# Three attention chunks in step, reordered loads, masks ahead of low parts, late conversions behind a fixed unit

## The chip, the cores and the metric

The kernel runs on one core of a Trainium2 chip. A core has five engines that run their own instruction streams and wait for each other by semaphores: TensorE (PE, matrix multiplications into accumulation banks), VectorE (DVE), ScalarE (ACT), GpSimd (POOL) and SyncE (SP, which here issues the transfers). The metric is device time in microseconds (us) of one launch; the kernel before takes 869.1 us, the median of three runs (868.42 to 871.12).

## The reference

Three stages follow one another, all in f32:

```python
f = 1 / (1 + exp(-f_logit))                     # 4 x 8 heads, 768 steps, 48 dims
for t in range(S):
    state = f[:, :, t, :, None] * state + einsum('bhd,bhe->bhde', k_t, v_t)
    y[:, :, t] = einsum('bhd,bhde->bhe', q_t, state)
x = y as 3072 tokens x 384
h = x @ w_in                                    # 384 -> 2048
x = where(h > 0, h, exp(min(h, 0)) - 1) @ w_out # 2048 -> 384
out = ((x @ w1) * (x @ w2) @ w3) @ w_out2       # 384 -> 1024 -> 1024 -> 384
```

Weights and inputs reach the kernel as 64-bit floats, in pairs of 32-bit words, and are converted on the chip.

## The kernel before

**Tiles.** The gated linear attention is cut into 24 chunks of 128 tokens (6 a batch), the first MLP into 8 tiles of 384 tokens, three chunks a tile. A tile has 16 *units* m, one for each 128 of the 2048 hidden columns; unit U = 16 j + m. In the order of the program, unit U holds `p1_split` of the unit before (the high part gh on ScalarE, L658, and the low part gl on VectorE, L659), the in-matmuls `p1_in` (9 in tiles 1 to 7, L640), the ELU (ScalarE L643 and L644, VectorE L646 into g) and the out-matmuls `p1_out` of unit U - 2 (9 or more, L672; after unit 15 the results leave by L681). Tile 0 runs in plain f32, the others as products of high and low parts.

**Attention.** Attention of tile j + 1 runs inside tile j. A chunk passes through the steps a_clamp, b0 to b5 and a4: clamp (L332), log of the gate (L351, L352), scan (L357), exponentials (L364, L365), scaling of key and query (L373, L374, on GpSimd for chunks 1 and 2) and a copy of the decay (L375), scores (L383) and transposes of the key (L389) on TensorE, masks on VectorE (L397, twice a chunk) and the copy of the transposed key on ScalarE (L399), then the output (L444), its high and low part (L453, L455) and the state (L408, L422 to L428). `ATT_AT` and `ATT_OFF` say at which units of the tile the three chunks' steps stand: masks in units 6, 10 and 14, the output right behind the in-matmuls of the same unit. For tile 0 `ATT_AT0` and `ATT_OFF0` do the same. The chunks of tile 0 itself are done in the prologue, in the order of `PRO_ORDER`: a code is the chunk and its step (k the last one), w a number of warm-up multiplications of zeros, j a conversion step. `PRO_LOADS` gives the order of the loads there on SP (l weights, d query and key, v values).

**Conversions.** A weight piece is loaded into a staging tile (wst, four buffers, L492), its magnitude is summed on ScalarE (L226, `cv_abs`), VectorE rebuilds the word (L230, L231, L236), and high and low part are split off. Conversions of w3 and w_out2 for the second MLP are spread over units 32 to 104 and go out to memory (L554, L560, L562). Those of w1 and w2 are the late jobs, `job_12`, in tile 7, and reuse the tile wa7 of the spilled ones.

**What sets the order.** The prologue and the units from `MAN` = 17 to `MAN_B` = 110 are in the order in which the code is written; everywhere else a scheduler places each instruction when the tiles that it needs are ready by its own estimate, so that it may put a job's first instruction ahead of units that come before it in the code. Every engine runs its stream in order. The w_out product (`w_rows`, L725) follows from unit 117 on, its operands o2 and w3 loaded by SP (L703, L713) behind the late jobs' loads.

Of the kernel before, what the change touches and what calls it, by code (L numbers as in the profile page):

```python
# [9 lines left out]
F32 = mybir.dt.float32  # L10
F32R = mybir.dt.float32r
U32 = mybir.dt.uint32
# [28 lines left out]
CPT = TN // CH  # L41
NTILE = NT // TN
# [7 lines left out]
Y_ROUNDS = ((0, 0, ((0, 0),)), (1, 64, ((80, 1),)), (2, 32, ((32, 0), (48, 1))))  # L50
ATT_AT = (0, 4, 8)
ATT_OFF = (0, 1, 2, 3, 4, 5, 6, 6)
ATT_AT0 = (0, 5, 9)
ATT_OFF0 = (0, 0, 1, 2, 3, 3, 4, 5)
ST_BUFS = 4
EARLY = (0, 1, 2, 3, 4, 6)
P2_Q = 1
SPILL_AT = 2 * MF
PRO_LOADS = "l d0 d1 l v0 v1 d2 l l v2 l l l"
PRO_ORDER = "w19 00 10 01 02 11 12 03 13 04 20 14 21 05 22 15 23 0k 1k j 06 j 16 24 25 2k 26"  # L60
BANKS = ("aaaaa", "hh0aa", "12aaa")
MAN = 17
Q_POOL = (1, 2)
# [184 lines left out]
def main_path(ctx, tc, flag, qkf, vin, w_in, w_out, w1, w2, w3T, w_out2, ident_d, tri_d, x2_scr, o2_scr, w3_scr, out):  # L248
    nc = tc.nc
# [3 lines left out]
    wp = ctx.enter_context(tc.tile_pool(name="wp", bufs=1))  # L253
# [13 lines left out]
    keep = tri_f.bitcast(U32).unsqueeze(1).to_broadcast([128, NP, CH])  # L267
# [21 lines left out]
    def carve(name, dt, *cols):  # L289
        t = wp.tile([128, KD * 512], dt, name=name)  # L290
        o = np.cumsum((0,) + cols)
        return [t[:, int(a):int(b)] for a, b in zip(o, o[1:])]

    def by_pair(t):
        return t.rearrange("r (p t) -> r p t", p=NP)
# [4 lines left out]
    for c, (x, y) in enumerate((("wb4", "wb5"), ("wb6", "wb7")), 1):  # L300
        e, k = carve(x, F32, 512, 512)
# [4 lines left out]
    def buf(c, nm, make):  # L306
        return own[c][nm] if c < CPT and nm in own[c] else make()
# [35 lines left out]
    def khc(c):  # L343
        return buf(c, "kh", lambda: kh)

    def amats(c):
        return buf(c, "amat", lambda: amat)
# [43 lines left out]

    c_ps = {}

    def b5(c):
        ps = c_ps.pop(c)
        for e in range(2):
            nc.vector.copy_predicated(out=amats(c)[e], mask=keep, data=by_pair(ps[e]))  # L397
        if len(ps) > 2:
            nc.scalar.activation(out=khc(c).rearrange("t p r -> t (p r)"), in_=ps[2][:, 0:NP * PR], func=AF.Copy)  # L399

    def a4k(c):
        if c % CPB == CPB - 1:
            return
        v = cx[c]["v"]
        kp = bank(c, 4)
        for i in range(NP):
            for e, (r, cc) in enumerate(blocks):
                nc.tensor.matmul(kp[r, 2 * D * i:2 * D * (i + 1)][:, cc], lhsT=khc(c)[:, i, r],  # L408
                                 rhs=v[:, i, V_AT[e]:V_AT[e] + D], start=True, stop=True)
        c_kp[c] = kp  # L410
# [65 lines left out]
    late = {}  # L476
# [18 lines left out]
    def cv_abs():  # L495
        i = cv["abs"]
        if i < cv["load"]:
            cv["abs"] += 1
            n, _, dst, place = jobs[i]
            src = cvt[i][0][:, 0:n, :]  # L500
            if place is None:
                if "wt" not in late:
                    late["wt"] = wp.tile([128, 3 * 512], U32, name="wa7")
                x = i % 4
                t = late["wt"][:, 512 * x:512 * x + n] if x < 3 else cv_p.tile([128, 512], U32, name="wt")[:, 0:n]
            else:
                t, groups = place()
                src = src.rearrange("p (a n) two -> p a n two", a=groups)
            cvt[i] = (src, t)
            rebias(nc, src, t, total[:, i:i + 1])  # L510
# [8 lines left out]
    def cv_step(k=1):  # L519

        while cv["split"] < cv["main"]:
            cv_split()
        i = cv["main"]
        k = min(k, len(jobs) - i)
        while cv["load"] < i + k:
            cv_load()
        while cv["abs"] < i + k:
            cv_abs()
        cv["main"] += k
        rebiased_to_f32(nc, [cvt[x] for x in range(i, i + k)])  # L530
        while cv["load"] < min(i + k + ST_BUFS - 2 + (3 if i < 2 * MF - 8 else 0), len(jobs)):
            cv_load()
        while cv["abs"] < min(cv["load"], i + k + (2 if i < 2 * MF else 1)):
            cv_abs()
# [226 lines left out]
    for m in range(MF + LAG):  # L761
        if m < MF:
            job_1(m, 0)
        if m >= LAG:
            job_1(m - LAG, 1)
    for code in PRO_LOADS.split():
        if code == "l":
# [12 lines left out]
    def fill():  # L780
# [4 lines left out]
        quota[0] = 0  # L785

    steps = (a_clamp, b0, b1, b2, b3, b4, b5, a4)
    psteps = steps[1:] + (a5,)
    wt = acc_p.tile([128, 512], F32, name="acc2")
    for c in range(CPT):  # L790
        a_clamp(c)
    for code in PRO_ORDER.split():
        if code[0] == "w":
            for _ in range(int(code[1:])):
                nc.tensor.matmul(wt[:, 0:128], lhsT=zero[:, 0:128], rhs=zero[:, 0:128], start=True, stop=True)
        elif code in "jJ":
            cv_step(1 + (code == "J"))
        else:
            psteps["0123456k".index(code[1])](int(code[0]))
    a_load(CPT)  # L800
# [9 lines left out]

    at_slots = [slots(ATT_AT0, ATT_OFF0), slots(ATT_AT, ATT_OFF)]
    lows = [(4 * q + i, o) for q in range(MF // 4) for o in range(2) for i in range(4)]
    for U in range(NU + LAG):
        j, m = divmod(U, MF)
        if U == MAN:
            man.enter_context(tc.manual_schedule())
        if U == MAN_B:
            man.close()
        if j == 0:
            while cv["main"] < at_job[0, m]:  # L820
                cv_step()
            quota[0] = T0_JOBS
        while lows and 2 * MF - len(lows) < 2 * (U - MF) + 4:
            low(*lows.pop(0))
        if U == SPILL_AT:
            start_spill()
        if SPILL_AT <= U < SPILL_AT + 3 * 3 * M2:
            spill_step(U - SPILL_AT, True)
            quota[0] = SPILL_AT - U - 1
        elif U >= SPILL_AT and cv["split"] < len(jobs):  # L830
            quota[0] = 1
        if U >= 1:
            p1_split(U - 1)
        todo = at_slots[j > 0].get(m, []) if j < NTILE - 1 else []
        for early in (1, 0):
            for i, k in todo:
                if (k in EARLY) == early:
                    c = CPT * (j + 1) + i
                    steps[k](c)
                    if k == len(steps) - 1:  # L840
                        a_load(c + 2)
            if early and U < NU:
                p1_in(U, fill)
        if j == 0 and m >= LAG:
            while cv["main"] < at_job[1, m - LAG]:
                cv_step()
        p1_out(U - LAG)
        while quota[0] > 0:
            fill()
        if j == NTILE - 2 and m == LATE_AT:  # L850
            start_late()
        if j == NTILE - 1 and m % 4 == 3:
            for a in range(KD):
                job_12(m // 4, a)
        r = U - ((NTILE - 1) * MF + 3 + LAG)
        if 0 <= r < M2:
            if r:
                w3_load(r + 1)
            w_rows(r)
        if m == 10 and j == NTILE - 1:  # L860
            p2_load(0)
        if m == 14 and j == NTILE - 1:
            p2_split(0)
# [57 lines left out]
    for U in range(N2 + LAG):  # L921
        j, m = divmod(U, M2)
# [87 lines left out]
```

## Time and profile before

| | us |
|---|---|
| median of three runs | 869.1 |
| profiled execution, its own time | 869.29 |
| its span on the core | 867.4 |
| TensorE busy | 844.8 |
| VectorE busy | 477.0 |
| ScalarE busy | 412.7 |
| GpSimd busy | 25.9 |

The span runs from the first to the last recorded instruction; the own time holds 1.9 us around it. An engine's busy time is the sum of its instructions; when it idles, the trace names what ended the wait. The granted TensorE clock has two levels, 1.2 GHz (0.5 in the profile) and 2.4 GHz (1.00); its mean over the span is 0.992.

### The profile page before, as it was taken

What the parts mean: (1) busy time and instruction counts of PE and PEld (TensorE: products, weight loads), DVE (VectorE), ACT (ScalarE), POOL (GpSimd) and SP (SyncE); (2) the same over time, 40 slices, a digit from 0 to 9 for tenths busy, and PEclk for the clock granted to TensorE, in tenths of its full rate; (3) what the DMA queues carried; (4) which work ended last, traced back from release to release, by engine and by line L of the source; (5) the groups of instructions that cost most, each with busy time, mean ns of one, the idle gap of its engine ahead of it and who ended that gap; (6) DMA issues with size and microseconds to landing.
All of it is one profiled execution on the core that took longest, in us unless ns stands there. A gap on an engine that the chain in (4) does not pass through costs nothing.

```text
span 867.4 us, 14383 instructions
## 1 busy us (share of the span) xinstructions
PE 844.8 (97%) x5768; PEld 742.8 (86%) x5768; DVE 477.0 (55%) x958; ACT 412.7 (48%) x863; POOL 25.9 (3%) x44
## 2 busy tenths in 40 slices
PE   7899999999999999999999999999999999999996
PEld 7566799989989999989889999988888888888885
DVE  7999388577577677677775552642323232222221
ACT  5886455566666665665664642531313222221211
POOL 3000000000000000001000000000000000000000
PEclk8999999999999999999999999999999999999999
DMA  9873211443444534445550765220201101000101
GB/s 274 261 239 114 67 47 44 134 116 112 145 128 141 168 115 129 157 139 177 167 164 22 305 199 172 85 64 1 73 1 37 37 0 37 1 36 1 37 1 40
DMA packets 47178, 90.79 MB, mean 105 GB/s; under 512 B 4144, under 2 KB 26928, under 8 KB 46848
## 3 DMA queue, kind: packets, MB, share of 16 engines
q1 hardware_dynamic: 47104, 89.80, 33.3%
q8 instruction: 47, 0.77, 0.4%
q14 instruction: 27, 0.22, 0.1%
HBM read 68.81 MB, written 20.97 MB: 104 GB/s over the span
## 4 chain that ended last, share of the span: by engine, by line
PE 85%; DVE 5%; ACT 4%; DMA 3%; issue 1%; SPq 0%; POOL 0%; ACTq 0%; DVEq 0%; POOLq 0%
PE acc L672 20%; PE h L640 19%; PE h L883 11%; PE at L883 11%; PE acc L909 11%; PE at L444 4%; PE at L725 4%; PE at L383 2%; PE at L408 1%; ACT gh L658 1%; PE at L389 1%; DMA qkf<-qkf_dram 1%; DMA wst<-moe_w_dram 1%; DMA wst<-moe_w_out_dram 1%; DVE g L646 1%
## 5 line engine op out<-in xcount | busy, mean ns | idle before, releaser
L672 PE MATMUL acc<-gh,wa 128*128 128x384 f32 x432 | 146.8, 370 | 0.0
L891 DVE TENSOR_TENSOR a<-at,a 128x512 f32<-128x512 f32 x48 | 33.2, 692 | 179.5 <-PE at L883 179.5
L640 PE MATMUL h<-xh,wa 128*128 128x384 f32 x348 | 117.9, 377 | 2.8 <-DVE gh L646 1.7
L672 PE MATMUL acc<-gh,wb 128*128 128x384 f32 x336 | 116.5, 348 | 2.1 <-ACT o L681 2.1
L640 PE MATMUL h<-xh,wb 128*128 128x384 f32 x336 | 113.2, 337 | 0.0
L672 PE MATMUL acc<-gl,wb 128*128 128x384 f32 x336 | 112.7, 336 | 0.0
L640 PE MATMUL h<-xl,wb 128*128 128x384 f32 x336 | 112.3, 334 | 0.0
L643 ACT ACTIVATE r<-h 128x384 f32<-128x384 f32 x128 | 62.0, 484 | 94.9 <-PE h L640 94.3
L646 DVE SCALAR_TENSOR_TENSOR g<-r,h 128x384 f32<-128x384 f32 x112 | 61.8, 552 | 74.8 <-ACT r L644 74.8
L672 PEld LDWEIGHTS acc<-gh,wa 128*128 128x128 f32 x432 | 80.9, 188 | 11.0 <-issue 0.2
L659 DVE TENSOR_TENSOR gl<-g,gh 128x384 fp32r<-128x384 f32 x112 | 62.6, 559 | 45.7 <-ACT gh L658 44.7
L658 ACT ACTIVATE gh<-g 128x384 fp32r<-128x384 f32 x112 | 58.6, 523 | 53.0 <-DVE g L646 52.2
L889 ACT ACTIVATE a<-h 128x512 f32<-128x512 f32 x48 | 28.7, 597 | 114.1 <-PE h L883 114.1
L640 PEld LDWEIGHTS h<-xh,wa 128*128 128x128 f32 x348 | 65.4, 188 | 15.8 <-DVE gh L646 2.3
L644 ACT ACTIVATE r<-r 128x384 f32<-128x384 f32 x128 | 67.1, 524 | 3.6
L672 PEld LDWEIGHTS acc<-gh,wb 128*128 128x128 f32 x336 | 63.2, 188 | 4.9 <-ACT o L681 2.7
L672 PEld LDWEIGHTS acc<-gl,wb 128*128 128x128 f32 x336 | 63.3, 189 | 0.1
L640 PEld LDWEIGHTS h<-xh,wb 128*128 128x128 f32 x336 | 63.1, 188 | 0.4
L640 PEld LDWEIGHTS h<-xl,wb 128*128 128x128 f32 x336 | 63.1, 188 | 0.4
L883 PE MATMUL h<-wb,wb 128*128 128x512 f32 x144 | 56.1, 390 | 0.0
L883 PE MATMUL h<-wa,wb 128*128 128x512 f32 x144 | 56.0, 389 | 0.0
L883 PE MATMUL at<-wa,wb 128*128 128x512 f32 x144 | 56.0, 389 | 0.0
(152 smaller groups left out, 1494.7 us busy)
## 6 DMA issues: line engine op xcount, KB each, us to landing
qkf<-qkf_dram SPq DMA_DIRECT2D x21, 672.0 KB, 5.8
wst<-moe_w_out_dram SPq DMA_DIRECT2D x24, 384.0 KB, 3.8
wst<-moe_w_dram SPq DMA_DIRECT2D x16, 512.0 KB, 4.2
wst<-moe_w_in_dram SPq DMA_DIRECT2D x16, 384.0 KB, 4.7
wst<-moe_w_dram SPq DMA_DIRECT2D x24, 256.0 KB, 3.8
v<-vin_dram SPq DMA_DIRECT2D x23, 224.0 KB, 5.7
out_dram<-wa SPq DMA_DIRECT2D x18, 256.0 KB, 2.1
w_scr<-wst SPq DMA_DIRECT2D x16, 256.0 KB, 2.1
```

What stands on the lines that cost most here:

```text
L444: nc.tensor.matmul(yp[32 * i:32 * i + 32, a * CH:(a + 1) * CH], lhsT=w[:, i, w0:w0 + 32], rhs=x[:, i, :], start=(n == 0), stop=(n == len(o ...
L640: nc.tensor.matmul(hp, lhsT=lw, rhs=rx, start=(n == 0), stop=(n == len(ops) - 1))
L643: nc.scalar.activation(out=r, in_=hp, func=AF.Relu, scale=-1.0)
L644: nc.scalar.activation(out=r, in_=r, func=AF.Exp, scale=-1.0)
L646: nc.vector.scalar_tensor_tensor(out=g, in0=r, scalar=-1.0, op0=ALU.add, in1=hp, op1=ALU.max)
L658: nc.scalar.activation(out=gh, in_=g, func=AF.Copy)
L659: nc.vector.tensor_tensor(out=gl, in0=g, in1=gh.bitcast(F32), op=ALU.subtract)
L672: nc.tensor.matmul(accs[j][i], lhsT=lw[:, 0, c], rhs=rg, start=(m == 0 and n == 0), stop=(m == MF - 1 and n == len(ops) - 1))
L725: nc.tensor.matmul(p, lhsT=lw[:, k, :], rhs=ro[:, k, :], start=(n == 0), stop=(n == 3 * M2 - 1))
L883: nc.tensor.matmul(p, lhsT=lw[:, a, e, c], rhs=rx[:, a, :], start=(n == 0), stop=(n == 3 * KD - 1))
L891: nc.vector.tensor_tensor(out=cc, in0=ps[1], in1=av, op=ALU.mult)
L909: nc.tensor.matmul(accs[j][i], lhsT=lw[:, m % 4, c], rhs=rc, start=(m == 0 and n == 0), stop=(m == M2 - 1 and n == 2))
```

## The change

In the prologue the query and key loads of chunks 0 and 1 come ahead of the first weights, the warm-ups are 28 instead of 19, the steps of the three chunks follow each other more closely, and the codes of conversion steps are set differently (`a` issues the magnitude sums alone). In tile 0 the attention of tile 1 starts one unit later. The step b5 is cut in two: masks (`b5m`) and key copy (`b5k`); from tile 1 on the masks stand ahead of `p1_split`. At unit 110 a new tile in the place of wa7 is made and one column of each of its thirds is set to zero by VectorE, so that no instruction on that tile can be placed ahead of it.

```diff
@@ -50,14 +50,14 @@
 Y_ROUNDS = ((0, 0, ((0, 0),)), (1, 64, ((80, 1),)), (2, 32, ((32, 0), (48, 1))))
 ATT_AT = (0, 4, 8)
 ATT_OFF = (0, 1, 2, 3, 4, 5, 6, 6)
-ATT_AT0 = (0, 5, 9)
+ATT_AT0 = (1, 6, 10)
 ATT_OFF0 = (0, 0, 1, 2, 3, 3, 4, 5)
 ST_BUFS = 4
 EARLY = (0, 1, 2, 3, 4, 6)
 P2_Q = 1
 SPILL_AT = 2 * MF
-PRO_LOADS = "l d0 d1 l v0 v1 d2 l l v2 l l l"
-PRO_ORDER = "w19 00 10 01 02 11 12 03 13 04 20 14 21 05 22 15 23 0k 1k j 06 j 16 24 25 2k 26"
+PRO_LOADS = "d0 d1 l v0 d2 v1 l v2 l l l l"
+PRO_ORDER = "w28 00 10 20 01 02 11 12 03 04 21 22 a 13 14 05 23 15 0k 24 25 1k j 06 16 26 2k"
 BANKS = ("aaaaa", "hh0aa", "12aaa")
 MAN = 17
 Q_POOL = (1, 2)
@@ -391,12 +391,18 @@
 
     c_ps = {}
 
-    def b5(c):
+    def b5m(c):
+        for e in range(2):
+            nc.vector.copy_predicated(out=amats(c)[e], mask=keep, data=by_pair(c_ps[c][e]))
+
+    def b5k(c):
         ps = c_ps.pop(c)
-        for e in range(2):
-            nc.vector.copy_predicated(out=amats(c)[e], mask=keep, data=by_pair(ps[e]))
         if len(ps) > 2:
             nc.scalar.activation(out=khc(c).rearrange("t p r -> t (p r)"), in_=ps[2][:, 0:NP * PR], func=AF.Copy)
+
+    def b5(c):
+        b5m(c)
+        b5k(c)
 
     def a4k(c):
         if c % CPB == CPB - 1:
@@ -793,8 +799,10 @@
         if code[0] == "w":
             for _ in range(int(code[1:])):
                 nc.tensor.matmul(wt[:, 0:128], lhsT=zero[:, 0:128], rhs=zero[:, 0:128], start=True, stop=True)
-        elif code in "jJ":
-            cv_step(1 + (code == "J"))
+        elif code == "j":
+            cv_step()
+        elif code == "a":
+            cv_abs()
         else:
             psteps["0123456k".index(code[1])](int(code[0]))
     a_load(CPT)
@@ -815,6 +823,8 @@
         if U == MAN:
             man.enter_context(tc.manual_schedule())
         if U == MAN_B:
+            late["wt"] = wp.tile([128, 3 * 512], U32, name="wa7")
+            nc.vector.memset(late["wt"].bitcast(F32).rearrange("p (x n) -> p x n", x=3)[:, :, 0:1], 0.0)
             man.close()
         if j == 0:
             while cv["main"] < at_job[0, m]:
@@ -829,14 +839,17 @@
             quota[0] = SPILL_AT - U - 1
         elif U >= SPILL_AT and cv["split"] < len(jobs):
             quota[0] = 1
+        todo = at_slots[j > 0].get(m, []) if j < NTILE - 1 else []
+        masks = [CPT * (j + 1) + i for i, k in todo if steps[k] is b5 and j > 0]
+        for c in masks:
+            b5m(c)
         if U >= 1:
             p1_split(U - 1)
-        todo = at_slots[j > 0].get(m, []) if j < NTILE - 1 else []
         for early in (1, 0):
             for i, k in todo:
                 if (k in EARLY) == early:
                     c = CPT * (j + 1) + i
-                    steps[k](c)
+                    (b5k if steps[k] is b5 and c in masks else steps[k])(c)
                     if k == len(steps) - 1:
                         a_load(c + 2)
             if early and U < NU:
```

Line numbers behind the new functions are 6 higher in most places after (g is L652, gh L664, gl L665, masks L396, key copy L401).

VectorE's stream in the prologue, from the end of chunk 0's preparation: wb is chunk 1 or 2's data, eq and ek the exponentials, amat and wb117 the masked scores. Before:

```order
L373 TENSOR_TENSOR qkf<-qkf,wb_116 112x512
L375 COPY dall<-wb_116 112x4
L357 SCALAR_TENSOR_TENSOR wb_114<-wb_114,cmax 112x128 x4
L397 COPY_PREDICATED amat_110<-tri_f,at 128x512
L397 COPY_PREDICATED amat_111<-tri_f,at 128x512
L397 COPY_PREDICATED wb_117<-tri_f,h 128x512 x2
L373 TENSOR_TENSOR wb_114<-wb_114,wb_118 112x512
L375 COPY dall<-wb_118 112x4
L426 TENSOR_TENSOR state_113<-at,dall 48x4x48 x2
L422 TENSOR_TENSOR state_112<-at,state_113 48x4x48 x2
L428 TENSOR_TENSOR state_112<-state_112,dall 48x4x48 x2
```

After:

```order
L357 SCALAR_TENSOR_TENSOR wb_114<-wb_114,cmax 112x128 x4
L373 TENSOR_TENSOR qkf<-qkf,wb_116 112x512
L375 COPY dall<-wb_116 112x4
L396 COPY_PREDICATED amat_110<-tri_f,at 128x512
L396 COPY_PREDICATED amat_111<-tri_f,at 128x512
L373 TENSOR_TENSOR wb_114<-wb_114,wb_118 112x512
L375 COPY dall<-wb_118 112x4
L396 COPY_PREDICATED wb_117<-tri_f,h 128x512 x2
L432 TENSOR_TENSOR state_113<-at,dall 48x4x48 x2
L396 COPY_PREDICATED wb_119<-tri_f,acc_276 128x512
L396 COPY_PREDICATED wb_119<-tri_f,acc_277 128x512
```

The scan of chunk 2 (L357 on wb) moved ahead of the multiplication of chunk 1's key, and the masks of chunk 2 (wb_119) ahead of the state.

Further on, where the first ELU result (L646, in after L652, gh) stands among the conversions (L230, L231, L236 on wa). Before:

```order
L357 SCALAR_TENSOR_TENSOR qkf<-qkf,cmax 112x128 x4
L230 TENSOR_SCALAR wa_311<-wa_311 128x384
L236 SCALAR_TENSOR_TENSOR wa_280<-wst_146,wa_280 128x3x128
L231 SCALAR_TENSOR_TENSOR wa_311<-wst_148,wa_311 128x384
L230 TENSOR_SCALAR wa_463<-wa_463 128x3x128
L236 SCALAR_TENSOR_TENSOR wa_311<-wst_148,wa_311 128x384
L231 SCALAR_TENSOR_TENSOR wa_463<-wst_150,wa_463 128x3x128
L373 TENSOR_TENSOR qkf<-qkf,ek 112x512
L646 SCALAR_TENSOR_TENSOR gh<-r,h 128x384
```

After:

```order
L428 TENSOR_TENSOR state_113<-at,state_112 48x4x48 x2
L230 TENSOR_SCALAR wa_236<-wa_236 128x3x128
L236 SCALAR_TENSOR_TENSOR wa_433<-wst,wa_433 128x384
L231 SCALAR_TENSOR_TENSOR wa_236<-wst_146,wa_236 128x3x128
L357 SCALAR_TENSOR_TENSOR qkf<-qkf,cmax 112x128
L236 SCALAR_TENSOR_TENSOR wa_236<-wst_146,wa_236 128x3x128
L357 SCALAR_TENSOR_TENSOR qkf<-qkf,cmax 112x128 x2
L652 SCALAR_TENSOR_TENSOR gh<-r,h 128x384
L357 SCALAR_TENSOR_TENSOR qkf<-qkf,cmax 112x128
```

The result comes behind three of the four pieces of the next tile's scan and ahead of conversions and a key multiplication that it followed.

VectorE at a unit with masks, here unit 6 of tile 3 (g, gl: ELU result and its low part; qkf: the next chunk). Before:

```order
L646 SCALAR_TENSOR_TENSOR g<-r,h 128x384
L659 TENSOR_TENSOR gl<-g,gh 128x384
L397 COPY_PREDICATED amat_110<-tri_f,at 128x512
L397 COPY_PREDICATED amat_111<-tri_f,at 128x512
L357 SCALAR_TENSOR_TENSOR qkf<-qkf,cmax 112x128 x4
L236 SCALAR_TENSOR_TENSOR wt<-wst,wt 128x384
L646 SCALAR_TENSOR_TENSOR g<-r,h 128x384
L455 TENSOR_TENSOR xl<-at,xh 128x3x128
```

After:

```order
L652 SCALAR_TENSOR_TENSOR g<-r,h 128x384
L396 COPY_PREDICATED amat_110<-tri_f,at 128x512
L396 COPY_PREDICATED amat_111<-tri_f,at 128x512
L665 TENSOR_TENSOR gl<-g,gh 128x384
L357 SCALAR_TENSOR_TENSOR qkf<-qkf,cmax 112x128 x4
L236 SCALAR_TENSOR_TENSOR wt<-wst,wt 128x384
L652 SCALAR_TENSOR_TENSOR g<-r,h 128x384
L461 TENSOR_TENSOR xl<-at,xh 128x3x128
```

The two masks changed places with the low part.

ScalarE in tile 6, up to the output copy o (wa with total: the magnitude sum of a conversion). Before:

```order
L658 ACTIVATE gh<-g 128x384
L226 ACTIVATE wa_1757,total<-wst 128x512
L643 ACTIVATE r<-h 128x384
L644 ACTIVATE r<-r 128x384
L554 ACTIVATE wst<-wa_1757 128x512
L658 ACTIVATE gh<-g 128x384
L351 ACTIVATE qkf<-qkf 112x512
L352 ACTIVATE qkf<-qkf 112x512
L643 ACTIVATE r<-h 128x384
L644 ACTIVATE r<-r 128x384
L226 ACTIVATE wa_1757,total<-wst 128x512
L681 ACTIVATE o<-acc_4078 128x384
```

After:

```order
L664 ACTIVATE gh<-g 128x384
L649 ACTIVATE r<-h 128x384
L650 ACTIVATE r<-r 128x384
L560 ACTIVATE wst<-wa_1766 128x512
L664 ACTIVATE gh<-g 128x384
L351 ACTIVATE qkf<-qkf 112x512
L352 ACTIVATE qkf<-qkf 112x512
L649 ACTIVATE r<-h 128x384
L650 ACTIVATE r<-r 128x384
L226 ACTIVATE wa_1766,total<-wst 128x512
L687 ACTIVATE o<-acc_4087 128x384
L687 ACTIVATE gc<-acc_4089 128x384
```

The first sum, of a late job, is gone here; the second belongs to a conversion that is spilled and stays.

VectorE at unit 110, in after, where the late jobs now begin (wa_5363 is the new tile):

```order
L665 TENSOR_TENSOR gl<-g,gh 128x384
L652 SCALAR_TENSOR_TENSOR g<-r,h 128x384
L827 MEMSET wa_5363 128x3
L396 COPY_PREDICATED amat_110<-tri_f,at 128x512
L396 COPY_PREDICATED amat_111<-tri_f,at 128x512
L665 TENSOR_TENSOR gl<-g,gh 128x384
L230 TENSOR_SCALAR wa_5363<-wa_5363 128x512 x2
L231 SCALAR_TENSOR_TENSOR wa_5363<-wst,wa_5363 128x512 x2
L236 SCALAR_TENSOR_TENSOR wa_5363<-wst,wa_5363 128x512 x2
L652 SCALAR_TENSOR_TENSOR g<-r,h 128x384
L230 TENSOR_SCALAR wa_5363<-wa_5363 128x512
```

Behind the low part and ahead of the next g stand now two conversions of three instructions each. In before the stretch is:

```order
L659 TENSOR_TENSOR gl<-g,gh 128x384
L646 SCALAR_TENSOR_TENSOR g<-r,h 128x384
L397 COPY_PREDICATED amat_110<-tri_f,at 128x512
L659 TENSOR_TENSOR gl<-g,gh 128x384
L397 COPY_PREDICATED amat_111<-tri_f,at 128x512
L646 SCALAR_TENSOR_TENSOR g<-r,h 128x384
L659 TENSOR_TENSOR gl<-g,gh 128x384
```

## Rows read from the trace of the kernel before

**Rows 1.** The page: busy time of the engines, and GB/s in 40 slices.
```profile
PE 844.8 (97%) x5768; PEld 742.8 (86%) x5768; DVE 477.0 (55%) x958; ACT 412.7 (48%) x863; POOL 25.9 (3%) x44
...
GB/s 274 261 239 114 67 47 44 134 116 112 145 128 141 168 115 129 157 139 177 167 164 22 305 199 172 85 64 1 73 1 37 37 0 37 1 36 1 37 1 40
```

**Rows 2.** Timeline, TensorE: start us, length, line, tiles, count, [wait before, releaser].
```profile
1.34 7.02 PE L795 MATMUL acc<-wb 128*128 128x128 f32 x38 [1.34 <-DVE cmax L772]
...
11.29 1.16 PE L383 MATMUL at<-qkf 48*128 48x128 f32 x16 [2.93 <-DVE qkf L374]
...
28.05 4.14 PE L640 MATMUL h<-xh,wa 128*128 128x384 f32 x12 [1.10 <-ACT xh L453]
...
33.85 2.20 PE L640 MATMUL h<-xh,wa 128*128 128x384 f32 x6 [1.66 <-DVE gh L646]
```

**Rows 3.** Timeline, VectorE in the prologue, columns as above.
```profile
9.94 0.69 DVE L373 TENSOR_TENSOR qkf<-qkf,ek 112x512 f32<-112x512 f32 x1 [0.52 <-DMA qkf<-qkf_dram]
...
12.20 1.24 DVE L375 COPY dall<-wb 112x4 f32<-112x4 f32 x1
...
13.35 1.36 DVE L357 TENSOR_TENSOR_SCAN wb<-wb,cmax 112x128 f32<-112x128 f32 x4
...
20.26 0.75 DVE L230 TENSOR_SCALAR wa<-wa 128x384 uint32<-128x384 uint32 x2
...
32.06 0.55 DVE L231 SCALAR_TENSOR_TENSOR wa<-wst,wa 128x384 uint32<-128x384 uint32 x1
...
32.52 0.68 DVE L373 TENSOR_TENSOR qkf<-qkf,ek 112x512 f32<-112x512 f32 x1
...
33.24 0.56 DVE L646 SCALAR_TENSOR_TENSOR gh<-r,h 128x384 f32<-128x384 f32 x1
```

**Rows 4.** Timeline, GpSimd in the prologue.
```profile
11.64 1.77 POOL L374 TENSOR_TENSOR qkf<-qkf,wb 112x512 f32<-112x512 f32 x1 [7.07 <-DMA qkf<-qkf_dram]
```

**Rows 5.** Windows of units: length; busy us (count) per engine; clock, DMA share, GB/s.
```profile
120.49:125.38 4.89, 4.89 (x68) 4.27 (x68) 4.83 (x13) 3.00 (x7) 0.00 (x0) 1.00 0.51 143
...
182.87:189.70 6.83, 5.97 (x91) 4.92 (x91) 5.60 (x13) 4.09 (x11) 0.00 (x0) 1.00 0.52 126
...
200.74:206.25 5.51, 5.51 (x92) 5.01 (x91) 5.37 (x13) 3.38 (x8) 0.55 (x2) 1.00 0.26 61
...
245.45:251.50 6.05, 5.11 (x68) 4.30 (x68) 5.34 (x13) 3.79 (x9) 0.00 (x0) 1.00 0.49 151
...
308.18:314.44 6.26, 5.96 (x92) 4.90 (x92) 5.59 (x13) 4.58 (x11) 0.16 (x1) 1.00 0.21 74
...
356.05:359.17 3.12, 3.12 (x20) 3.12 (x19) 2.36 (x7) 2.95 (x7) 0.00 (x0) 1.00 0.63 224
...
418.75:423.77 5.02, 3.42 (x20) 3.10 (x19) 3.27 (x8) 4.91 (x12) 0.00 (x0) 1.00 0.85 262
...
435.34:444.60 9.26, 7.49 (x91) 6.21 (x91) 8.52 (x18) 5.81 (x14) 1.21 (x2) 0.82 0.42 120
```

**Rows 6.** Timeline, unit 6 of tile 3: VectorE, then ScalarE.
```profile
246.68 0.56 DVE L659 TENSOR_TENSOR gl<-g,gh 128x384 fp32r<-128x384 f32 x1 [0.59 <-ACT gh L658]
...
247.16 1.33 DVE L397 COPY_PREDICATED amat<-tri_f,at 128x512 f32<-128x512 uint32 x2
...
246.56 0.53 ACT L399 ACTIVATE kh<-at 128x448 f32<-128x448 f32 x1
```

**Rows 7.** Timeline, tile 6: ScalarE once, then TensorE twice.
```profile
415.93 0.66 ACT L226 ACTIVATE wa<-wst 128x512 f32<-128x512 f32 x1 [2.58 <-DMA wst<-moe_w_dram]
...
422.08 0.44 PE L672 MATMUL acc<-gh,wb 128*128 128x384 f32 x1 [1.60 <-ACT o L681]
...
438.55 0.43 PE L444 MATMUL at<-qkf,state 112*32 112x128 f32 x8 [1.49 <-ACT kh L399]
```

**Rows 8.** Timeline, w_out product: SP's queue, then TensorE.
```profile
475.39 0.33 SPq L703 DMA_DIRECT2D o2h<-o_scr  x1
...
498.68 1.55 PE L725 MATMUL at<-o2h,w3h 128*128 128x384 f32 x8
```

## The prediction

> **What bounds the kernel now.** I read the page's busy line first: TensorE is busy 844.8 of 867.4 us, VectorE 477.0 [rows 1]. So the time is TensorE's work and its few waits, and an edit off TensorE counts only where TensorE waits for it. Next I read the timeline of TensorE's first 40 us: after the warm-up multiplications it waits 2.93 us for the first query tensor, and later 1.10 us and 1.66 us; from 33.85 us on it no longer waits [rows 2]. Then the timeline of the other engines there: of the VectorE rows only that at 9.94 us has a wait before it [rows 3], so the prologue ends when VectorE is through. Then windows, one per MLP unit: a unit of a kind shows the same TensorE work in each tile, so its excess length is a wait [rows 5]. Last the timelines inside three of the long units [rows 6, 7] and around the w_out product [rows 8].
>
> **Prologue (loads, 28 warm-ups, order of three chunks).** TensorE's first run without a wait begins when the first g, on VectorE at 33.24 us, frees the hidden buffer that the second batch needs, at 33.85 us [rows 2, 3]. What precedes that g in VectorE's order sets it. Counted in the two orders, seven instructions fewer stand ahead of it now: two L230 at 0.75 / 2 us, two L231 at 0.55, one L236 of the same tile shape, taken at 0.55 too, one piece of a scan at 1.36 / 4, one multiplication L373 at 0.68 [rows 3]. That is 0.75 + 1.10 + 0.55 + 0.34 + 0.68 = 3.42 us. Back to back each begins some 0.09 us before the one ahead has ended (32.06 + 0.55 against 32.52), so 2.8 us net. The chunk-2 masks and state that now come ahead of the first conversion come behind it in before, and ahead of g in both: no difference. The loads: VectorE waits 0.52 us at 9.94 us for a query and key load [rows 3]; with 384 KB of weights no longer ahead of it on SP this may go, worth 0 to 0.5 us. The weights land later, but their first reader on VectorE stands at 20.26 us. The nine more warm-ups add 9 x 7.02 / 19 = 3.3 us to a stretch that ended at 8.36 us; the first scores start at 11.29 us [rows 2], so they may start 0.3 to 0.4 us later, while VectorE is busy with its own scans until 13.35 + 1.36 us [rows 3] ahead of the masks that read them. Attention in tile 0 is put one unit later; TensorE does not wait there in before, and each g of tile 0 comes earlier than it did, so I price it at nothing; should that cover go, the price is one g, about 0.6 us a unit. I take 3.2 us, between 2.8 and 3.9. The bounds are -1 (scores late, all else equal) and 4.5 (also the 1.10 us wait for xh gone).
>
> The one place where the new order can lose this: scan 2 now stands ahead of the key multiplication, beside GpSimd's query multiplication. In before the copy of 112x4 there took 1.24 us, and ended with GpSimd's 1.77 us instruction at 13.4 us [rows 3, 4]; VectorE was held. The Trainium skill ("SBUF — State Buffer", section "Who interferes with whom") says that a VectorE instruction with two SBUF inputs and a GpSimd instruction that reads SBUF exclude one another, the one that starts first holding the port to its end. The trace agrees as far as that row goes. By that rule the scan would now be held in the copy's place, the copy no longer, and the prologue would give 2.0 to 2.4 us instead of 3.2 if more than the copy's wait is lost.
>
> **Masks ahead of the low parts (units 6, 10, 14 of tiles 2 to 5).** Nothing is added; g, gl, masks becomes g, masks, gl. In tile 3 the low part waits for its high part until 246.68 us and the two masks run only then, 247.16 to 248.49 us, while TensorE's 9 in-matmuls have ended about 247.0 [rows 6]. Placed behind g, which ends 246.1, they end about 247.4: some 1.1 us earlier. What the stalls cost: tile 3, unit 6, is 6.05 us against 4.89 us for the like unit of tile 1: 1.16. Tile 2 has 6.83 and tile 4 6.26 against 5.51 for the same matmuls without a stall: 1.32 and 0.75. The like unit of tile 5 repeats tile 3's, 1.16 [rows 5]. Sum 4.4 us. The key copy on ScalarE ends at 247.09 us [rows 6] and stays, so some 0.1 to 0.4 us of each unit remains: I take 3.5 us of 4.4. Bounds 0 (the copy or the scan rules) and 4.4. The low part comes up to 0.75 us later; its reader, the out-matmuls, runs a unit or more afterwards, with 9 in-matmuls of 3.12 us a unit [rows 5] between: nothing. If that cover goes, 0.75 us for 12 units, 9 us.
>
> **Late conversions held behind unit 110.** In tile 6 four of them lie between attention's steps. ScalarE stands at the first for 2.58 us, for a load of staging, at 415.93 us [rows 7]; everything on ScalarE queues behind it, and TensorE waits 1.60 us at 422.08 us for the output copy. That unit is 5.02 us against 3.12 us in tile 5: 1.90. The unit at 435.34 us is 9.26 us at a granted clock of 0.82 against 5.51 us at 1.00: 3.75 us [rows 5], begun by a wait of 1.49 us at 438.55 us [rows 7], with masks and key copy behind a conversion on each engine. Together 5.65 us; I take 5.5, with bounds 0 and 6.2. What is moved still has to run: the first two jobs' three pairs of VectorE instructions now stand between gl and g of unit 110. From the 128x384 rows, scaled by 512 / 384, a job is (0.38 + 0.55 + 0.55) x 4 / 3 = 2.0 us, an estimate; two are 4 us ahead of one g, whose out-matmuls come two units on, 6.2 us. It fits; otherwise up to 2 us is given back. The new memset waits for an earlier store of the same tile that left in tile 6: nothing. From the w_out product on, the order of every engine is the old one.
>
> SP is passed too: the staging buffers are freed only at unit 110, and the loads of the last late jobs wait for that on SP, with the loads of o2 and w3 behind them. In before these left at 475.39 us and the product began at 498.68 us [rows 8]. Its first group needs 1536 + 1536 + 512 + 512 KB = 4.19 MB, at the 305 GB/s of that slice [rows 1] 13.8 us, so landed by 489.2: 9.5 us to spare. Now four conversion steps (4 us), four issues and 1 MB (3.4 us) may stand ahead: about 8.8 us in the worst case. It just fits, at nothing.
>
> **Sum.** 3.2 + 3.5 + 5.5 = 12.2 us off the profiled execution's own 869.29 us: 857.1. That execution lies 0.2 us above the median of the runs, so 857.0.
>
> **Rivals.**
> 1. The late conversions are not what holds tile 6: the wait for the staging load moves to the spill conversion behind it, and the clock falls as before. For it: the load's queue is busy there; against: that conversion, next on ScalarE, did not wait. Then 869.3 - 6.7 = 862.6 us. Chance 0.12.
> 2. The prologue gives nothing, since VectorE runs into the later weights, or tile 0, where it is busy throughout, gives the gain back. Then 860.3 us. Chance 0.13.
> 3. The port: scan 2 held by GpSimd for up to the 1.24 us of the row. Then 858.0 to 858.3 us. Chance 0.10.
> 4. The masks give nothing since key copy or scan end last. Then 860.6 us. Chance 0.06.
> 5. Slower, or no change: SP holds o2 and w3 back. The place is the product's first group, the price one us for each us that their issue falls behind 475.39 + 9.5 = 484.9 us (on before's time scale); from 497 us on it eats the whole gain. For it: SP issues in order and the new wait stands ahead; against: the conversions that free the buffers start at unit 110, about where the loads left in before. At 490 us it gives 862, at 497 us 869, at 500 us 872. Chance 0.10, with 0.05 for within 0.3% and 0.04 beyond it.
>
> **Numbers.** The forecast, 857.0 us, has 0.49; its own range is 854 to 860. The range for 8 in 10 reaches up to rival 1 and down to the upper bounds (4.5 + 4.4 + 6.2 = 15.1 off): 853.5 to 863. A gain or loss of 0.3%, 2.6 us, is what a measurement of this kernel can tell from none. Faster 0.91, within 0.3% 0.05, slower 0.04.
>
> **What would show it.** In the changed profile: the second batch of tile 0 starts near 30.6 us instead of 33.85, and TensorE does not wait until tile 2; the scores start by 11.7 us; the units of tiles 2 to 5 listed above are 5.0 to 5.6 us long, with at most 0.4 us idle ahead of the attention output; ScalarE shows no conversion wait in tile 6, and its unit 6 is under 6 us at clock 1.00; the product starts without a wait some 12 us before 498.68. I am wrong if a wait of over 1 us stands in tile 0 behind a g, if TensorE waits for the key copy where it waited for the masks, or if the product's start shows a DMA as its releaser.

## The result and the profile after

The changed kernel takes 856.7 us (median of four runs, 855.45 to 857.38), the kernel before 870.0 us beside it: a ratio of 0.9847, 95% interval 0.9824 to 0.9870. Forecast were 857.0 us. The profiled execution took 856.14 us, its span 854.3 us. In the page's busy line TensorE lost 2.6 us of work and, of its idle time, 10.5 us [rows 1]. No work was taken out (there are 18 records more), so the 2.6 us are matrix multiplications that ran faster; the mean granted clock over the span is 0.995, in before 0.992:

```profile
PE 842.2 (99%) x5786; PEld 743.8 (87%) x5786; DVE 476.0 (56%) x959; ACT 413.6 (48%) x863; POOL 24.4 (3%) x44
```

The prologue of the changed kernel, in the timeline, TensorE first, then VectorE, then GpSimd; these rows answer to [rows 2 to 4]:

```profile
1.33 8.44 PE L801 MATMUL acc<-wb 128*128 128x128 f32 x56 [1.33 <-DVE cmax L778]
...
10.70 1.16 PE L383 MATMUL at<-qkf 48*128 48x128 f32 x16 [0.93 <-DVE qkf L374]
...
31.48 2.20 PE L646 MATMUL h<-xh,wa 128*128 128x384 f32 x6 [1.38 <-DVE gh L652]
...
10.63 2.39 DVE L357 TENSOR_TENSOR_SCAN wb<-wb,cmax 112x128 f32<-112x128 f32 x4
...
14.83 1.34 DVE L373 TENSOR_TENSOR wb<-wb,wb 112x512 f32<-112x512 f32 x1
...
10.72 1.40 POOL L374 TENSOR_TENSOR qkf<-qkf,wb 112x512 f32<-112x512 f32 x1 [6.14 <-ACT wb L365]
```

The second batch starts at 31.48 us, 2.37 us earlier. The scan of chunk 2 takes 2.39 us beside GpSimd's 1.40 us instruction, where four pieces took 1.36 us, and the next key multiplication 1.34 us beside GpSimd's next one (14.35 us, 1.28 us long).

The windows of units 6 of tiles 2, 3 and 4, and of units 2, 6 and 10 of tile 6 (columns as in [rows 5]):

```profile
180.08:185.86 5.78, 5.56 (x91) 5.02 (x91) 5.16 (x12) 3.71 (x10) 0.00 (x0) 1.00 0.59 151
...
241.61:246.55 4.94, 4.94 (x68) 4.27 (x67) 4.85 (x12) 3.33 (x8) 0.00 (x0) 1.00 0.66 186
...
303.16:308.67 5.51, 5.51 (x92) 5.01 (x91) 5.44 (x13) 4.50 (x11) 0.09 (x1) 1.00 0.24 81
...
411.82:414.94 3.12, 3.12 (x20) 3.12 (x20) 2.32 (x6) 2.67 (x7) 0.00 (x0) 1.00 0.88 264
...
425.97:431.74 5.77, 5.59 (x92) 5.05 (x92) 5.27 (x13) 3.93 (x9) 0.00 (x0) 1.00 0.44 121
...
442.77:448.61 5.84, 5.59 (x92) 5.05 (x91) 5.54 (x14) 4.12 (x10) 0.43 (x1) 1.00 0.28 93
```

Tile 3 is at 4.94 us, without a wait, and unit 6 of tile 6 at 5.77 us and clock 1.00, after 9.26 us at 0.82. Over the span, the lead of each unit's start over that of before grows by 2.37 us up to tile 1, 0.4 in unit 2 of tile 2, 4.1 in unit 6 of tiles 2 to 5, and 5.6 in tile 6, 12.5 us in all. The 0.4 us are no gain that is shown: that unit takes 3.12 to 4.73 us in the executions of this case, whatever the part. The product starts 12.54 us earlier, and the output's tail takes 0.6 us less.

What stands around tile 6 and the product now, in the timeline: ScalarE, TensorE, SP's queue, TensorE.

```profile
440.06 0.68 ACT L226 ACTIVATE wt<-wst 128x512 f32<-128x512 f32 x1 [2.39 <-DMA wst<-moe_w_dram]
...
427.87 0.42 PE L450 MATMUL at<-qkf,state 112*32 112x128 f32 x8 [0.18 <-DVE amat L396]
...
436.19 27.12 SPq L498 DMA_DIRECT2D wst<-moe_w_dram  x6
...
463.72 0.33 SPq L709 DMA_DIRECT2D o2h<-o_scr  x1
...
486.14 1.55 PE L731 MATMUL at<-o2h,w3h 128*128 128x384 f32 x8
```

The wait of 1.49 us ahead of the attention output has become 0.18 us, and none over 0.3 us is left on TensorE between 32 us and the end. ScalarE still waits 2.39 us for staging in tile 6, where the prediction expected none, but in unit 9. SP stands 27 us at the late loads, and o2 leaves at 463.72 us, 0.9 us later than in before if counted from the product's start; the product does not wait.

### The profile page after: what moved, and what is told of

Its sections match the earlier page's. It is cut to its first block, busy times and chain, and to the rows that moved or that the text cites. A ratio compares the mean times of both kernels' runs of the same rounds, so it can differ in the third digit from the quotient of the medians.

```text
span 854.3 us, 14396 instructions
## 1 busy us (share of the span) xinstructions
PE 842.2 (99%) x5786; PEld 743.8 (87%) x5786; DVE 476.0 (56%) x959; ACT 413.6 (48%) x863; POOL 24.4 (3%) x44
## 4 chain that ended last, share of the span: by engine, by line
PE 89%; DVE 4%; ACT 3%; DMA 2%; issue 1%; SPq 0%; ACTq 0%
PE acc L678 21%; PE h L646 20%; PE h L896 11%; PE acc L922 11%; PE at L896 11%; PE at L731 4%; PE at L450 4%; PE at L383 2%; PE at L414 1%; PE at L389 1%; DVE qkf L357 1%; ACT gh L664 1%; DVE g L652 1%; DMA wst<-moe_w_out_dram 1%; DMA w_scr<-wst 1%
## 5 line engine op out<-in xcount | busy, mean ns | idle before, releaser
L646 PE MATMUL h<-xh,wa 128*128 128x384 f32 x348 | 118.0, 377 | 1.5 <-DVE gh L652 1.4
L646 PE MATMUL h<-xh,wb 128*128 128x384 f32 x336 | 113.2, 337 | 0.0
L646 PE MATMUL h<-xl,wb 128*128 128x384 f32 x336 | 112.3, 334 | 0.0
L652 DVE SCALAR_TENSOR_TENSOR g<-r,h 128x384 f32<-128x384 f32 x112 | 61.7, 551 | 73.6 <-ACT r L650 73.5
L664 ACT ACTIVATE gh<-g 128x384 fp32r<-128x384 f32 x112 | 58.6, 523 | 53.0 <-DVE g L652 51.4
L665 DVE TENSOR_TENSOR gl<-g,gh 128x384 fp32r<-128x384 f32 x112 | 62.3, 556 | 38.8 <-ACT gh L664 38.4
L646 PEld LDWEIGHTS h<-xh,wa 128*128 128x128 f32 x348 | 65.4, 188 | 14.4 <-DVE gh L652 2.2
L646 PEld LDWEIGHTS h<-xl,wb 128*128 128x128 f32 x336 | 63.1, 188 | 0.4
L646 PEld LDWEIGHTS h<-xh,wb 128*128 128x128 f32 x336 | 63.1, 188 | 0.4
```

The source lines that it names most:

```text
L646: nc.tensor.matmul(hp, lhsT=lw, rhs=rx, start=(n == 0), stop=(n == len(ops) - 1))
L652: nc.vector.scalar_tensor_tensor(out=g, in0=r, scalar=-1.0, op0=ALU.add, in1=hp, op1=ALU.max)
L664: nc.scalar.activation(out=gh, in_=g, func=AF.Copy)
L665: nc.vector.tensor_tensor(out=gl, in0=g, in1=gh.bitcast(F32), op=ALU.subtract)
```

## The experiments

**Each part alone.** Three kernels take the kernel before and one part of the change each: masks and `b5m` / `b5k`; the new tile with its memset; or the prologue's tables with `ATT_AT0`. In short:

```diff
 masks_only:    + masks ahead of p1_split for units of tile 1 on
 late_only:     + late["wt"] = wp.tile(...); nc.vector.memset(...) at U == MAN_B
 prologue_only: + PRO_LOADS, PRO_ORDER, ATT_AT0 and the code "a" of the changed kernel
```

> The kernel before with the masks ahead of the low part and nothing else. Theory (the parts are separate, each paying in its own units): unit 6 of tiles 2, 3, 4 and 5 becomes shorter by 1.0 to 1.2 us, 0.75 in tile 4, 4.1 us in all as in the changed kernel; in tile 6, where a late conversion still stands ahead, 0 to 0.5 us; the time is 865 to 866 us against 869 to 870. Rival (key copy or scan end last without the other parts): these units keep their length and the time stays above 868.5 us.

> The kernel before with the new tile and its memset at unit 110 and nothing else. Theory: units 2 and 6 of tile 6 lose their stalls (1.9 us and 3 to 3.7 us; of the second some 0.5 us may stay, since the masks are still behind the low part), in all 5 us, and the time is 864 to 865.5 us. Rival (the wait for staging only moves to the spill conversion): ScalarE waits some 2 us ahead of the next L226 in tile 6, at most 2.5 us are gained, and the time is 867 us or more.

> The kernel before with the new order of loads, the 28 warm-ups, the new order of the prologue and attention of tile 1 one unit later, and nothing else. Theory: the second batch of in-matmuls starts at 31.5 us, all later units keep their length, and the time is 867 to 868 us. Rival (the gain of 2.4 us needs the other parts, or tile 0 gives it back): tile 1 starts within 1 us of the time before, 99.0 us.

Measured, as ratios to before at 870.7 us on the same chip: masks 0.9935 (0.9914 to 0.9957), 865.4 us; late conversions 0.9972 (0.9953 to 0.9992), 868.0 us; prologue 0.9945 (0.9928 to 0.9961), 865.5 us. The product of the three is 0.985, the whole change's 0.9847: within these intervals the parts add up. They are not the sizes that were expected: 5.7 us (3.7 to 7.5), 2.4 us (0.7 to 4.1) and 4.8 us (3.4 to 6.3) by these ratios. The first expectation's total held, the second's fell (864 to 865.5), the third gained more (867 to 868); its second batch starts at 30.42 us and its tile 1 at 95.59, in before at 33.85 and 99.02.

Window of unit 6 of tile 6, masks alone, with TensorE's wait in it from the timeline:

```profile
433.91:441.01 7.10, 5.59 (x91) 5.05 (x91) 6.11 (x14) 4.98 (x13) 0.00 (x0) 1.00 0.41 121
...
437.14 0.43 PE L450 MATMUL at<-qkf,state 112*32 112x128 f32 x8 [1.51 <-DVE amat L396]
```

Units 2, 6 and 10 of tile 6, late conversions alone, with ScalarE's wait ahead of unit 10:

```profile
421.45:424.57 3.12, 3.12 (x19) 3.12 (x19) 2.32 (x6) 2.68 (x7) 0.00 (x0) 1.00 0.89 254
...
435.61:442.39 6.78, 5.97 (x91) 4.92 (x91) 5.66 (x14) 4.25 (x9) 0.16 (x1) 1.00 0.35 97
...
453.43:460.47 7.04, 5.96 (x92) 4.90 (x92) 6.12 (x14) 4.62 (x10) 0.54 (x2) 1.00 0.24 77
...
450.93 0.67 ACT L226 ACTIVATE wt<-wst 128x512 f32<-128x512 f32 x1 [2.60 <-DMA wst<-moe_w_dram]
```

In before these units take 5.02, 9.26 [rows 5] and 5.51 us:

```profile
455.64:461.15 5.51, 5.51 (x92) 5.01 (x91) 4.54 (x11) 2.96 (x6) 0.56 (x2) 1.00 0.10 38
```

So of the 3.75 us that unit 6 lost, masks alone take 2.2 us back, the held conversions alone 2.5, both 3.5. But with masks alone TensorE still waits 1.51 us there, where it waited 1.49 us in before [rows 7]: what came back is mostly the granted clock, 1.00 instead of 0.82. And that the change need not have brought back. The prologue alone leaves tile 6 as it was, and there TensorE waits 1.49 us too, yet the clock stays at 1.00. Its unit 6:

```profile
432.13:439.86 7.73, 5.96 (x91) 4.90 (x91) 7.12 (x16) 5.21 (x13) 0.14 (x1) 1.00 0.36 100
```

So 1.5 of the 9.26 us belong to one execution of before. Against 7.73 us, masks alone give 0.6 us in this unit, the held conversions alone 1.0, both 2.0. The whole of tile 6 (16 units) in before, with the prologue alone, masks alone, late conversions alone, and in the changed kernel:

```profile
412.51:479.96 67.45, 63.62 (x546) 59.86 (x546) 45.66 (x94) 38.67 (x82) 2.42 (x4) 0.97 0.41 127
```

```profile
407.86:475.22 67.36, 62.38 (x546) 58.42 (x546) 45.67 (x94) 38.69 (x82) 2.42 (x4) 1.00 0.41 128
```

```profile
411.79:476.36 64.57, 61.70 (x545) 58.70 (x545) 45.24 (x94) 38.77 (x82) 2.42 (x4) 1.00 0.41 132
```

```profile
415.21:479.27 64.06, 62.16 (x545) 58.49 (x545) 45.29 (x95) 38.98 (x82) 2.42 (x4) 1.00 0.34 104
```

```profile
405.57:467.42 61.85, 61.42 (x546) 58.78 (x546) 44.95 (x95) 38.98 (x82) 2.42 (x4) 1.00 0.36 110
```

The tile is no shorter with the prologue alone: its units 1 and 2 are 1.4 us longer than in before, behind a wait of ScalarE for staging of 3.94 us instead of 2.58. Masks alone take 2.9 us off the tile, the held conversions alone 3.4, both 5.6. The held conversions do not come free: the fourth late conversion uses another tile (wt), which the memset does not hold. Its wait for staging, 2.60 us, comes now in unit 9, and unit 10 is 1.5 us longer. With the masks ahead, the same wait costs 0.3 us (5.84 against 5.51). The rival of the second expectation was right in that a wait for staging stays, and its 2.5 us is about what that part gained alone; but the wait stands ahead of a late conversion, and not of the spill conversion that it named.

**One late conversion let through.**

```diff
-            memset(late["wt"] ... [:, :, 0:1], 0.0)
+            memset(late["wt"] ... [:, 1:3, 0:1], 0.0)
```

> The changed kernel with the memset on the second and third part of the tile only, so that one late conversion may again be placed in tile 6: ScalarE's sum and VectorE's three instructions then stand in and about unit 6. Theory (each conversion in an attention unit delays masks and key copy by its own instructions, 0.7 us on ScalarE, 1.8 us on VectorE): unit 6 of tile 6 is 0.5 to 2 us longer than 5.77 us, unit 2 not, and the time is 857 to 858.7 us. Rival (the wait for the staging load alone made the stalls): both units keep their length of the changed kernel, and the time is that of it, 856.7 us.

Its units 6 and 10 of tile 6:

```profile
425.88:432.12 6.24, 5.58 (x91) 5.04 (x91) 5.65 (x14) 4.42 (x11) 0.00 (x0) 1.00 0.39 106
...
443.16:448.67 5.51, 5.51 (x92) 5.01 (x91) 5.23 (x13) 3.90 (x9) 0.49 (x1) 1.00 0.30 98
```

6.24 against 5.77 us, just under the low end of the expectation; but unit 10 is 0.33 us shorter, the ratio is 0.9846 (0.9829 to 0.9862), and the total is the changed kernel's. One conversion in an attention unit costs half a microsecond there. That in before several of them hurt, with a load that had not landed, is inferred: no run here separates the two.

**GpSimd out of the prologue.**

```diff
-Q_POOL = (1, 2)
+Q_POOL = ()
```

> The changed kernel with the query multiplications of chunks 1 and 2 on VectorE instead of GpSimd, so that GpSimd runs nothing beside the prologue's scan. Theory (VectorE is held while GpSimd works: the scan of chunk 2 took 2.39 us instead of 1.36, the key multiplication of chunk 2 1.34 instead of 0.67): the scan takes 1.4 us, that multiplication 0.7 us; two multiplications of 0.6 us come in, so the second batch starts 0.3 to 0.6 us earlier than 31.48, near 31.1, and the time is 856.2 to 856.6 us, no difference that the total can show. Rival (the scan is long for another reason, its data or its own waits): the scan stays at 2.4 us and the second batch starts near 32.7 us.

VectorE's scan of chunk 2, key multiplication of chunk 2, first conversion, and TensorE's second batch, from its timeline:

```profile
10.58 1.36 DVE L357 TENSOR_TENSOR_SCAN wb<-wb,cmax 112x128 f32<-112x128 f32 x4
...
14.35 0.67 DVE L373 TENSOR_TENSOR wb<-wb,wb 112x512 f32<-112x512 f32 x1
...
20.41 0.75 DVE L230 TENSOR_SCALAR wa<-wa 128x384 uint32<-128x384 uint32 x2
...
30.35 2.20 PE L646 MATMUL h<-xh,wa 128*128 128x384 f32 x6 [1.87 <-DVE gh L652]
```

The time is 855.6 us, the ratio 0.9840 (0.9817 to 0.9863). Scan and multiplication are back at 1.36 and 0.67 us: GpSimd had held VectorE for 1.03 and 0.67 us. The Trainium skill's rule ("SBUF — State Buffer", section "Who interferes with whom") states just that for a VectorE instruction with two SBUF inputs beside a GpSimd one that reads SBUF. The trace agrees: the scan has two (its data and cmax) and was held. The second batch starts 1.1 us earlier than in the changed kernel's profile. Whether that is the port had to be seen with the two side by side:

> The changed kernel itself, once more, to be set against the next one on the same chip. Theory: 856 to 857.5 us, its second batch at 31.0 to 32.0 us, since nothing in its prologue waits for the loads of query and key. Rival (the prologue hangs on transfers in the changed kernel too): the second batch moves by more than 1 us from 31.48.

> The changed kernel with the query multiplications of the prologue on VectorE, once more, beside the changed kernel on the same chip. Theory: the second batch is 1.1 us earlier, so the median is 0.7 to 1.3 us below that of the changed kernel. Rival: the gain of the prologue is lost in the scatter of the runs, the medians differ by under 0.4 us.

The ratios are 0.9847 (0.9826 to 0.9869) for the changed kernel and 0.9845 (0.9823 to 0.9867) for this one: no difference; the expectation of a gain fell. In its second profile the changed kernel's second batch starts at 30.35 us too, 1.13 us from the first, where at most 0.5 us had been expected. The windows of 14 to 21 us show a reason: first the changed kernel's first profile, then its second, then the changed kernel with GpSimd's work on VectorE, second profile, from 30.5 to 34 us (the number ahead of the last two is the granted clock).

```profile
14.00:21.00 7.00, 6.75 (x92) 5.69 (x93) 6.20 (x13) 3.46 (x11) 1.28 (x1) 0.62 1.09 356
```

```profile
14.00:21.00 7.00, 6.18 (x146) 5.32 (x146) 6.81 (x15) 4.74 (x15) 1.28 (x1) 1.00 1.08 352
...
30.35 2.20 PE L646 MATMUL h<-xh,wa 128*128 128x384 f32 x6 [1.45 <-DVE gh L652]
```

```profile
30.50:34.00 3.50, 3.23 (x6) 1.81 (x7) 3.50 (x10) 2.12 (x7) 0.00 (x0) 0.65 0.75 265
...
30.77 3.50 PE L646 MATMUL h<-xh,wa 128*128 128x384 f32 x6 [1.96 <-DVE gh L652]
```

The same kernel ran the prologue's attention at a mean clock of 0.62 once, with the level of 1.2 GHz in it, and at 1.00 the other time; VectorE's waits for TensorE of 0.25 and 0.46 us in the first are gone in the second. The batch moved by 1.1 us. In the third row the clock falls after a wait of 1.96 us, and six multiplications take 3.50 us instead of 2.20. So the port's share is at most the 0.4 us between the first conversions (20.82 in the changed kernel's second profile, 20.41 here), and the scatter hides it.

**The three tables of the prologue, each set back in the changed kernel.**

```diff
 warm19:    -PRO_ORDER = "w28 ..."        +PRO_ORDER = "w19 ..."
 old_loads: -PRO_LOADS = "d0 d1 l v0 ..." +PRO_LOADS = "l d0 d1 l v0 ..."
 att0_old:  -ATT_AT0 = (1, 6, 10)         +ATT_AT0 = (0, 5, 9)
```

> The changed kernel with the 19 warm-ups of before. Theory: TensorE idles from about 7 us to 10.7 us and then runs the prologue's scores and outputs at the lower granted clock, as in before; VectorE, which waits 0.25 and 0.46 us for scores and state in the changed kernel, then waits longer, and the second batch starts 0.3 to 1.5 us later than 31.48 us. Rival (VectorE sets the prologue whatever the clock): it starts within 0.2 us of 31.48 us.

> The changed kernel with the load order of before (weights ahead of query and key). Theory: VectorE waits again some 0.5 us for the first query and key, the later loads come as before, and the second batch starts 0.5 to 1 us later than 31.48 us. Rival (VectorE is busy anyway and takes the wait up): it starts within 0.2 us.

> The changed kernel with attention of tile 1 one unit earlier, as in before. Theory: the whole scan of the next tile comes ahead of the first g on VectorE, one piece of 0.34 us and a conversion more, so the second batch starts 0.3 to 0.9 us later than 31.48 us, and tile 1 as much later than 96.64 us. Rival: VectorE stands ahead of TensorE in tile 0, a g comes late with attention in unit 0, and tile 1 starts over 1.5 us later.

One run each: 857.9, 861.4 and 859.2 us, where the changed kernel's nine runs lie between 855.2 and 857.4. Their rows, in this order: 19 warm-ups (window, then the first scores and the second batch); old loads (key multiplications of chunks 0 and 2, the second batch); attention earlier (second batch, and two waits in tile 0).

```profile
14.00:21.00 7.00, 7.00 (x70) 5.91 (x71) 5.56 (x10) 2.26 (x7) 1.28 (x1) 0.50 1.08 354
...
10.71 1.16 PE L383 MATMUL at<-qkf 48*128 48x128 f32 x16 [2.42 <-DVE qkf L374]
...
32.52 2.20 PE L646 MATMUL h<-xh,wa 128*128 128x384 f32 x6 [1.25 <-DVE gh L652]
```

```profile
10.21 0.69 DVE L373 TENSOR_TENSOR qkf<-qkf,ek 112x512 f32<-112x512 f32 x1 [0.49 <-DMA qkf<-qkf_dram]
...
16.83 0.69 DVE L373 TENSOR_TENSOR wb<-wb,wb 112x512 f32<-112x512 f32 x1 [1.02 <-DMA wb<-qkf_dram]
...
34.25 2.20 PE L646 MATMUL h<-xh,wa 128*128 128x384 f32 x6 [1.62 <-DVE gh L652]
```

```profile
31.62 2.20 PE L646 MATMUL h<-xh,wa 128*128 128x384 f32 x6 [1.65 <-DVE gh L652]
...
80.31 2.20 PE L646 MATMUL h<-xh,wa 128*128 128x384 f32 x6 [1.70 <-DVE gh L652]
...
87.01 2.20 PE L646 MATMUL h<-xh,wa 128*128 128x384 f32 x6 [1.28 <-DVE gh L652]
```

With 19 warm-ups TensorE waits 2.42 us before the first scores, and the clock is 0.50 through the attention that follows; VectorE waits for it, and the second batch is 1.0 us later than in the changed kernel's slower profile, 2.2 us than in its faster one. With the old loads the batch is 2.8 us later or more, far over the 0.5 to 1 us expected, and tile 1 4.5 us. VectorE waits 0.49 and 1.02 us for loads there; but the clock from 14 to 21 us is 0.53 too, so that not all of the 2.8 us is shown to be the loads'. Attention one unit earlier does not move the second batch (31.62), against the theory, but then TensorE waits twice behind a g, 3.0 us in all, and tile 1 starts 3.7 us later than in the changed kernel: the rival.

> As the last one, and the first chunk of tile 1's attention one unit later still (2, 6, 10). Theory (the shift in tile 0 pays since it takes attention's VectorE work out of the units where VectorE is behind): ahead of the first g three scan pieces go (1.0 us), a clamp and two conversion instructions come (1.1 us), so the second batch stays within 0.3 us of 30.35, TensorE runs through tile 0 without a wait, and the time is that of the last one within 0.5 us. Rival (the step from 0 to 1 gave its gain by the place of the scan alone, and more shift gives more): the second batch starts 0.7 us earlier or more, with the total following.

A unit later still: ratio 0.9866 (0.9842 to 0.9889), so no further gain is shown that way. The second batch starts at 29.67 us, as the rival said, and a wait of 0.96 us behind a g in tile 0 takes it back.

**SP's queue.**

```diff
-MAN_B = 110
+MAN_B = 114
```

> The changed kernel with the hand-written order, the new tile and its memset ending four units later, at unit 114. This asks what the rival on SP's queue costs: the staging buffers are freed four units (some 14 us) later, so the loads of o2 and w3, which left at 463.72 us, leave near 477 us, while the product would start at 486.1 us. Theory (SP's order is a wait that only spare time hides): the first group needs 4.19 MB, 10 to 14 us at 300 to 410 GB/s, so it starts at 487 to 491 us and TensorE waits 1 to 5 us there. Rival (the loads do not wait for the conversions, or the held-back conversions stall units 114 to 117 instead): the product starts without a wait for a transfer.

```profile
463.78 0.33 SPq L709 DMA_DIRECT2D o2h<-o_scr  x1
...
487.07 1.55 PE L731 MATMUL at<-o2h,w3h 128*128 128x384 f32 x8
```

Inconclusive (one run, 857.8 us): the loads of o2 left when they did in the changed kernel, since in this order they stand ahead of the late loads that wait, and the product does not wait. What a late o2 would cost was not measured.

## Why the prediction was right, point by point

The time (857.0 against 856.7 us) and the sum (12.2 of 13.1 us between the profiles) were right. Place by place the terms fit as well: 2.4 us up to tile 1, 4.1 in tiles 2 to 5 and 5.6 in tile 6, for 3.2, 3.5 and 5.5. By part of the change they do not: each lies outside the interval that its part measured alone, the first two just, the third by far. That two terms too small and one too large make a right sum is in part luck, and in part one stall booked under the wrong part. (The lower end of the range, 853.5, is 0.5 us below what its own bounds give, 869.1 - 15.1 = 854.0; nothing hangs on it.)

- **Prologue, 3.2 us.** Between the profiles 2.37 us (3.50 with the changed kernel's second), alone 4.8 us by the ratio. The mechanism held: g bounds the second batch, and it comes earlier by the order. Rival 3 held in its mechanism and not in its time: scan and multiplication took 1.03 and 0.67 us longer, and the copy fell from 1.24 to 0.16 us. (The copy read for it has one SBUF input, so that row did not bear on a rule for two; the scan's does.) What I mis-sized is the prologue of before. It waits for loads and runs in part at the lower clock, and by how much differs between executions. The two kernels with a part alone and the old prologue show it; masks alone, then late conversions alone:

```profile
10.36 0.69 DVE L373 TENSOR_TENSOR qkf<-qkf,ek 112x512 f32<-112x512 f32 x1 [0.69 <-DMA qkf<-qkf_dram]
...
35.32 2.20 PE L646 MATMUL h<-xh,wa 128*128 128x384 f32 x6 [1.42 <-DVE gh L652]
```

```profile
10.51 0.69 DVE L373 TENSOR_TENSOR qkf<-qkf,ek 112x512 f32<-112x512 f32 x1 [1.05 <-DMA qkf<-qkf_dram]
...
35.83 2.20 PE L640 MATMUL h<-xh,wa 128*128 128x384 f32 x6 [1.42 <-DVE gh L646]
```

Same instructions, and 1.5 to 2 us later than 33.85 [rows 2]: the profiled execution of before (869.29 us, where the medians are 868.8 to 870.7) had a short prologue. The new prologue's second batch starts at 30.35, 30.42 (prologue alone), 31.48, 31.51 (`MAN_B` at 114) and 31.92 us (one conversion let through): 3.9 us earlier in the mean of five than in that of three, which agrees with the 4.8 us of the ratio (3.4 to 6.3). I read one execution's wait of 0.52 us as the price of the load order.
- **Attention in tile 0 one unit later, at nothing.** Wrong as a cost left out: with the shorter prologue the old place costs 3.7 us at tile 1, in one run, 3.0 of it in two waits. I had looked only at whether TensorE waits in before, where its late start left VectorE room; that cover goes with the gain.
- **28 warm-ups, at 0.3 to 0.4 us of delay that does not count.** The nine more took 1.4 us (8.44 against 7.02), not 3.3, and the first scores came at 10.70, not 11.6 us, since they wait for VectorE and not for the warm-ups. Their worth seems to be the clock behind them, which I had left out of the sum: 1 to 2 us at the second batch, from one run.
- **Masks, 3.5 us.** In tiles 2 to 5 4.1 us; almost nothing remains of the key copy's 0.1 to 0.4 us. Masks alone took another 2.9 us off tile 6, which I had put to the late conversions.
- **Late conversions, 5.5 us.** The step "begun by a wait of 1.49 us ... together 5.65 us" booked a stall with two causes on one, and 1.5 us of it, the clock of 0.82, on a cause that does not bring it each time. Alone they give 2.4 us by the ratio and 3.4 us in tile 6, since masks behind the low part still hold unit 6, and since the fourth conversion's wait for staging stays, in unit 9. That is rival 1 for one job in four, though ahead of a late conversion and not of the spill conversion, and with the clock at 1.00.
- **Given back at unit 110, and SP.** Nothing, as said: TensorE does not wait at units 110 to 112 or at the product.

## What to carry to other kernels

When several causes stand in one stall, the stall's length is not the worth of either: undo them one by one, or book the stall once for the set. A wait that an earlier stage does not have can be the slack which that stage's delay gives it; price a shift against the schedule after the other gains. Take a prologue that waits for loads, and a stall in which the clock fell, from several executions, not from one.

## What was not expected of the hardware

The granted clock differs between executions of the same instructions. From 14 to 21 us it is 0.50, 0.55, 0.63 and 0.67 in the four profiles with 19 warm-ups; with 28 it is 1.00 in six profiles and 0.53, 0.61, 0.62 and 0.63 in four. The wait ahead of the first scores does not part these ten (0.70 to 1.42 us where it was 1.00, none in one of them; 0.75 to 1.09 us where it was lower), and the rows do not say what does. In unit 6 of tile 6 it fell to 0.82 in before, after waits of 1.49 and 0.29 us, and stayed at 1.00 after the same two waits with the prologue alone. GpSimd's work held a VectorE scan for 1.03 us and a multiplication for 0.67 us, yet moving that work to VectorE changed no time.
